# Linear attention and a gated feed-forward block on one core: the first stage's loads reordered over two DMA queues, and a second x tile transposed on TensorE

## Chip, core and metric

The kernel runs on one core of a Trainium2 chip. The metric is the device time of one execution in microseconds. The times given for a kernel are the median of several executions and their lowest and highest; a profile is of one execution, and its span runs from the first to the last instruction.

## What is computed

x is 2048 x 640 in bf16 (2048 tokens, width 640). A linear attention with 32 heads of 20 columns and a feed-forward block with 1728 hidden columns both read x, and a gate per token mixes them.

```python
g = sigmoid((x * gate_w).sum(-1))
q, k, v = split(x @ wqkv)                  # 640 columns each, 32 heads of 20
phi = lambda t: where(t > 0, t + 1, exp(t)) + 1e-6
kv  = per head: phi(k)^T @ v               # 20 x 20
z   = per head: sum over tokens of phi(k)
a   = (phi(q) @ kv) / (phi(q) . z + 1e-6) @ wo
b   = (gelu(x @ w_gate) * (x @ w_up)) @ w_down
out = g * a + (1 - g) * b
```

## The kernel before

**Tiles.** The tokens are cut into NT = 16 tiles of 128, the width 640 into KC = 5 pieces of 128. TensorE needs x with the width on the partitions, and so a transposed copy, xT. The key and query projections multiply one 128 x 128 piece of xT with the 640 key columns (wk) or the 640 query columns (wq) of the same piece of width, and sum over the five pieces in PSUM. A 641st query column holds gate_w, so that the query projection gives the gate's sum too.

**Order of the work.** There is no scheduler: each engine runs its instructions in the order in which the program text names them (class `_Plan`), and the plan puts a semaphore wait ahead of an instruction where its operands need one. A wait holds up everything that stands behind it on the same engine. Loads are issued by the sequencers of SP (`eng="sp"`) and of ACT (`eng="act"`), and each has a DMA queue of its own: q1 for SP, q10 for ACT.

**First stage (lines 363 to 535).** NXN = 1 tile of x is loaded as it is (`load_x`, L343) and transposed by TensorE (`T`, L439: five transposes against an identity into PSUM, from where VectorE copies them into xT, L443). All other tiles come through transposing DMAs (`load_xT`, L355), which SP issues. The `load_wk` and `load_wq` loads (L343) bring 160 KB each. SP's order is: x 0, wk 0, xT 1, wk 3, wk 4, xT 2, xT 3, wq 0 to 4, xT 4 to 15, then the bulk loads (the remaining untransposed x, the feed-forward weights, wv, wo). ACT's order is: a load of 16 rows of 8 bytes (`touch`, L368), wk 1, wk 2, an Exp on one column that brings the activation table in (L379), and gate_w (L381).

TensorE first runs matmuls on constants (`warm`, L425). Then the NQ = 4 first tiles have key and query done in units of their own: `KM(n, ks)` (L459 and L460) multiplies pieces ks of key unit n, with 512 and 128 columns, `QM(n, ks)` (L474 and L475) those of a query unit, with 512 and 129. Unit n uses PSUM banks `slot(n)`: (0, 1), (2, 3), (4, 5), (6, 7) in turn. TensorE's order is

```python
warm(5, 512); warm(1, 128)
T(0, [0], 7); T(0, [1, 2, 3, 4], 6)
warm(2, 128)
KM(0, [0]), KM(0, [1]), KM(0, [2]), KM(1, [0]), KM(1, [1]), KM(1, [2])
KM(0, [3]), KM(1, [3]); gate_col(); KM(0, [4]), KM(1, [4])
KM(2, ALLK), KM(3, ALLK)       # then the query units of the tiles 0 to 3
```

`gate_col` is one small matmul (L504) that turns gate_w into a column and a copy by VectorE (L506) into column 641 of wq; every `QM` waits for that copy. After each unit `phi1` (ACT, L484 and L488) and `phi2` (VectorE, L494 and L498) apply phi and free the unit's banks.

**Key and query of the other tiles (L538 to 574).** `KQ(i)` multiplies the five pieces of xT tile i with wk and wq side by side in three groups (512, 512 and 257 columns, L545) into banks 0 to 2 or 3 to 5, for i from NQ to 15, with phi on ACT (L555) and VectorE (L561, L564).

**After that** TensorE sums phi(k)^T x over all tiles (L602 to L617), runs the feed-forward's gate and up products (L706) with the small attention matrices in between, and ends with the output products (L859, L880). These parts are the same in both kernels.

Of the kernel before, what the change touches and what calls it, by code (L numbers as in the profile page):

```python
# [6 lines left out]
ACT = mybir.ActivationFunctionType  # L7
ALU = mybir.AluOpType
BF16 = mybir.dt.bfloat16
F32 = mybir.dt.float32  # L10
# [5 lines left out]
NT = S // 128  # L16
KC = D // 128
# [3 lines left out]
EPS = 1e-6  # L21
XW = 656

NXN = 1
NQ = 4


class _Res:
# [134 lines left out]
def bass_gated_mix__linear_attn_block__geglu_ffn__prompt_kernel(  # L163
# [63 lines left out]
    with (  # L227
# [8 lines left out]
        with contextlib.ExitStack() as stack:  # L236
            dma_sems = [stack.enter_context(nc.semaphore("s_in%d" % i)) for i in range(n_dma_in)]

            P = _Plan(["pe", "act", "dve", "pool", "sp"])
# [9 lines left out]
            def new_dma_key():  # L249
                k = "in%d" % dma_next[0]  # L250
                dma_next[0] += 1
                return k

            def v16(o, n):
                return pool[:, o:o + n]

            def v32(o, n):
                return pool[:, o:o + 2 * n].bitcast(F32)
# [38 lines left out]
            eg = v32(O_EG, 16)  # L297
# [3 lines left out]
            gw_sb = v16(O_GW, 128)  # L301
# [6 lines left out]
            r_xT = [P.sb("xT%d" % i, R_XT, R_XT + KC * S) for i in range(NT)]  # L308
            r_xTa = [P.sb("xTa%d" % i, R_XT, R_XT + S) for i in range(NXN)]
            r_wk = [P.sb("wk%d" % k, R_WK + k * WW, R_WK + k * WW + 640) for k in range(KC)]  # L310
# [25 lines left out]
            r_eg = [P.res("eg%d" % i) for i in range(NT)]  # L336
# [3 lines left out]
            r_gw = P.res("gw")  # L340
# [7 lines left out]
            def load_x(i, eng="sp"):  # L348
                dma_in(x_aug[:, i, 0:640], A_x[0, i * 128:(i + 1) * 128, :], [r_xn[i]], eng=eng)

            def load_wk(k, eng="sp", after=()):
                dma_in(wk[:, k, :], A_wqkv[k * 128:(k + 1) * 128, 640:1280], [r_wk[k]], reads=after, eng=eng)

            def load_xT(i, after=()):
                P.op("sp", lambda e: e.dma_start_transpose(xT[:, :, i * 128:(i + 1) * 128],  # L355
                                                           A_x[0, i * 128:(i + 1) * 128, :]),
                     reads=list(after), writes=[r_xT[i]], dma=new_dma_key())

            def load_wq(k, eng="sp"):
                dma_in(wq[:, k, 0:640], A_wqkv[k * 128:(k + 1) * 128, 0:640], [r_wq[k]], eng=eng)  # L360
# [4 lines left out]
                                                   base=0, channel_multiplier=1),  # L365
                 reads=[r_ones], writes=[r_ident])
            P.op("pool", lambda e: e.memset(v32(R_WO, NHC * 320), 0.0), reads=[r_ident], writes=[r_woz] + r_wo)
            P.op("act", lambda e: e.dma_start(touch[0:16, 0:4], A_wqkv[0:128:8, 640:644]),  # L368
                 writes=[P.res("touch")], dma=new_dma_key())
            load_x(0)  # L370
            load_wk(0)
            load_xT(1)
            load_wk(3)
            load_wk(4)
            load_wk(1, "act")
            load_wk(2, "act")

            zero = nc.const_aps.tensor(0.0, (128, 1), F32)
            P.op("act", lambda e: e.activation(eg[:, 0:1], zero, ACT.Exp), writes=[r_eg[0]])  # L379
            P.op("dve", lambda e: e.memset(gw_sb, 0.0), writes=[r_gw])  # L380
            dma_in(gw_sb[0:5, :], gate_w.rearrange("(k p) -> k p", p=128), [r_gw], eng="act")  # L381
            for i in range(2, NQ):
                load_xT(i)
            for k in range(KC):
                load_wq(k)
            for i in range(NQ, NT):
                load_xT(i)
            dma_in(x_aug[:, NXN:8, 0:640],
                   A_x[0, NXN * 128:8 * 128, :].rearrange("(i p) w -> p i w", p=128), r_xn[NXN:8])
            dma_in(x_aug[:, 8:NT, 0:640],  # L390
# [30 lines left out]
            def warm(count, n):  # L421
                def fn(e):
                    last = None
                    for w in range(count):
                        last = e.matmul(ps[:, 4, 0:n], one_l, one_r[:, 0:n], start=True, stop=True)  # L425
                    return last
                P.op("pe", fn, writes=[bank[4]])
# [7 lines left out]
            def T(i, ks, tb):  # L435
                def fn(e):
                    last = None
                    for n, k in enumerate(ks):
                        last = e.transpose(psb[:, tb, n * 128:(n + 1) * 128],  # L439
                                           x_aug[:, i, k * 128:(k + 1) * 128], ident)  # L440
                    return last
                P.op("pe", fn, reads=[r_xn[i], r_ident], writes=[bank[tb]])
                P.op("dve", lambda e: e.tensor_copy(  # L443
                    xT[:, ks[0]:ks[-1] + 1, i * 128:(i + 1) * 128],
                    psb[:, tb, 0:len(ks) * 128].rearrange("p (k s) -> p k s", k=len(ks))),
                    reads=[bank[tb]], writes=[r_xTa[i] if ks[0] == 0 else r_xT[i]])


            seq = [("k", i) for i in range(NQ)] + [("q", i) for i in range(NQ)]

            def KM(n, ks):
                i = seq[n][1]
                b0, b1 = slot(n)

                def fn(e):
                    last = None
                    for k in ks:
                        lhs = xT[:, k, i * 128:(i + 1) * 128]
                        e.matmul(ps[:, b0, :], lhs, wk[:, k, 0:512], start=(k == 0), stop=(k == KC - 1))  # L459
                        last = e.matmul(ps[:, b1, 0:128], lhs, wk[:, k, 512:640],  # L460
                                        start=(k == 0), stop=(k == KC - 1))
                    return last
                P.op("pe", fn, reads=[r_xTa[i] if i < NXN and ks == [0] else r_xT[i]] + [r_wk[k] for k in ks],
                     writes=[bank[b0], bank[b1]])

            def QM(n, ks):
                i = seq[n][1]
                b0, b1 = slot(n)

                def fn(e):  # L470
                    last = None
                    for k in ks:
                        lhs = xT[:, k, i * 128:(i + 1) * 128]
                        e.matmul(ps[:, b0, :], lhs, wq[:, k, 0:512], start=(k == 0), stop=(k == KC - 1))  # L474
                        last = e.matmul(ps[:, b1, 0:129], lhs, wq[:, k, 512:641],  # L475
                                        start=(k == 0), stop=(k == KC - 1))
                    return last
                P.op("pe", fn, reads=[r_xT[i], r_gcol] + [r_wq[k] for k in ks],
                     writes=[bank[b0], bank[b1]])

            def phi1(n):
                b0, b1 = slot(n)
                m = n % 4
                P.op("act", lambda e: e.activation(e_buf[m], ps_flat[:, b0 * 512:b0 * 512 + 640], ACT.Exp),  # L484
                     reads=[bank[b0], bank[b1]], writes=[r_e[m]])
                kind, i = seq[n]
                if kind == "q":
                    P.op("act", lambda e: e.activation(eg[:, i:i + 1], ps[:, b1, 128:129], ACT.Tanh, scale=0.5),  # L488
                         reads=[bank[b1]], writes=[r_eg[i]])

            def phi2(n):
                b0, b1 = slot(n)
                m = n % 4
                P.op("dve", lambda e: e.tensor_scalar(e_buf[m], e_buf[m], 1.0, EPS, ALU.min, ALU.add),  # L494
                     reads=[r_e[m]], writes=[r_e[m]])
                kind, i = seq[n]
                dst, r_dst = (pk[i], r_pk[i]) if kind == "k" else (pq[i], r_pq[i])
                P.op("dve", lambda e: e.scalar_tensor_tensor(  # L498
                    dst, ps_flat[:, b0 * 512:b0 * 512 + 640], 1.0 + EPS, e_buf[m], ALU.add, ALU.max),
                    reads=[bank[b0], bank[b1], r_e[m]], writes=[r_dst])  # L500
# [10 lines left out]
            warm(1, 128)  # L511
            T(0, [0], 7)
            T(0, [1, 2, 3, 4], 6)
            warm(2, 128)
            for k in range(3):
                KM(0, [k])
            for k in range(3):
                KM(1, [k])
            KM(0, [3])
            KM(1, [3])  # L520
            gate_col()
            KM(0, [4])
            KM(1, [4])
            ALLK = list(range(KC))
            for n in range(2 * NQ):
                if n in (2, 3):
                    KM(n, ALLK)
                if n == NQ:
                    for k in ALLK:
                        QM(NQ, [k])  # L530
                        QM(NQ + 1, [k])
                if n > NQ + 1:
                    QM(n, ALLK)
                phi1(n)
                phi2(n)


            def KQ(i):  # L538
                b = 3 * (i % 2)
# [405 lines left out]
```

## Time and profile before

| | |
|---|---|
| time, median of 3 executions | 273.71 us (273.53 to 273.76) |
| the profiled execution, its own time | 273.49 us |
| its span | 272.2 us |
| VectorE (DVE) busy | 140.9 us, 52% of the span |
| ScalarE (ACT) busy | 76.0 us, 28% |
| GpSimd (POOL) busy | 30.6 us, 11% |
| moved by queue q1, which SP issues | 23.05 MB |
| moved by queue q10, which ACT issues | 0.33 MB |

What lies around the span is 273.49 - 272.2 = 1.3 us. PE stands for TensorE's matmuls, PEld for its weight loads, which go on beside the matmuls; SPq and ACTq are the sequencers of SP and ACT that issue DMAs. In a timeline a row has its start, its duration, engine, line, operation, output <- input, shapes and count; the bracket tells how long the engine had been idle before it and what ended that idle time. The start-to-start distance of two matmuls is the time that the first takes of TensorE's stream; the durations overlap. A DMA's time to landing is counted from its issue to the last of its completion signals.

### The profile page before, as it was taken

Reading aid. Unit: us, or ns where it says so; the run is one execution under the profiler, and the core shown is the slowest. Engines: PE = TensorE matmul, PEld = TensorE weight load, DVE = VectorE, ACT = ScalarE, POOL = GpSimd, SP = SyncE. Lnnn points to the kernel's source line nnn. Section 1 sums busy time; section 2 is a strip of 40 time slices with the busy share of each in tenths; the row PEclk is TensorE's granted clock in tenths of the full one; section 3 lists DMA queues with packets and bytes.
Section 4 is the critical chain, followed back from the end, with each engine's and each line's share of the span. In section 5 each row is a group of like instructions: output and inputs, shape, how many; then the busy total and the mean of one; then the engine's idle time right before and its main releaser. Section 6 shows DMA issues by size and latency. Waiting matters only on the chain.

```text
span 272.2 us, 3462 instructions
## 1 busy us (share of the span) xinstructions
PE 267.0 (98%) x1366; PEld 127.2 (47%) x1392; DVE 140.9 (52%) x248; ACT 76.0 (28%) x132; POOL 30.6 (11%) x30
## 2 busy tenths in 40 slices
PE   7999999999999999999999999999999999999997
PEld 3555555544445454444444444444444444444444
DVE  1678989997234335999999999634110000000200
ACT  2455555210422453332222232224011122121021
POOL 6000000003240002242332421000000000000000
DMA  7976999610200011614121221262031110110221
GB/s 192 203 117 120 356 401 379 117 3 19 58 19 2 23 52 48 198 28 52 24 48 29 46 48 25 60 233 94 2 78 40 39 39 19 41 39 19 58 60 39
DMA packets 42680, 23.61 MB, mean 87 GB/s; under 512 B 32167, under 2 KB 41255, under 8 KB 42535
## 3 DMA queue, kind: packets, MB, share of 16 engines
q1 hardware_dynamic: 42333, 23.05, 32.2%
q10 hardware_dynamic: 330, 0.33, 0.4%
q8 instruction: 11, 0.18, 0.3%
q14 instruction: 6, 0.05, 0.1%
HBM read 13.67 MB, written 2.63 MB: 60 GB/s over the span
## 4 chain that ended last, share of the span: by engine, by line
PE 96%; DMA 1%; SPq 1%; issue 1%; DVE 0%
PE ps L706 41%; PE ps L880 23%; PE ps L545 12%; PE ps L602 6%; PE ps L859 4%; PE ps L684 2%; PE ps L474 2%; PE ps L827 2%; PE ps L605 1%; DMA pool<-in_A_x_dram 1%; PE ps L459 1%; PE ps L840 1%; SPq L343 1%; SPq L355 0%; PE ps L755 0%
## 5 line engine op out<-in xcount | busy, mean ns | idle before, releaser
L706 PE MATMUL ps<-pool 128*128 128x512 bf16 x509 | 112.8, 379 | 0.7 <-issue 0.2
L706 PEld LDWEIGHTS ps<-pool 128*128 128x128 bf16 x520 | 50.6, 98 | 60.3
L880 PE MATMUL ps<-pool 128*128 128x512 bf16 (+2 forms) x300 | 62.2, 366 | 0.5 <-issue 0.2
L712 ACT ACTIVATE pool<-ps 128x512 f32<-128x512 f32 x52 | 31.1, 597 | 72.8 <-PE ps L706 70.1
L714 DVE TENSOR_TENSOR pool<-ps,pool 128x512 bf16<-128x512 f32 x52 | 34.7, 688 | 31.1 <-PE ps L706 29.8
L880 PEld LDWEIGHTS ps<-pool 128*128 128x128 bf16 x306 | 29.2, 98 | 33.4 <-issue 0.4
L863 DVE TENSOR_TENSOR pool<-ps,pool 128x512 bf16<-128x512 f32 x4 | 2.8, 692 | 61.5 <-PE ps L859 59.4
L545 PE MATMUL ps<-pool 128*128 128x512 bf16 (+1 forms) x176 | 32.5, 343 | 0.2
L770 POOL TENSOR_TENSOR pool<-pool 128x640 f32<-128x640 bf16 x16 | 22.5, 1406 | 72.6 <-DVE pool L772 65.8
L887 ACT ACTIVATE pool<-ps,pool 128x512 bf16<-128x512 f32 (+1 forms) x16 | 10.9, 681 | 68.6 <-PE ps L880 68.6
L545 PEld LDWEIGHTS ps<-pool 128*128 128x128 bf16 x180 | 17.6, 98 | 15.0
L564 DVE SCALAR_TENSOR_TENSOR pool<-ps,pool 128x128 bf16<-128x128 f32 (+2 forms) x36 | 21.7, 603 | 2.1
L555 ACT ACTIVATE pool<-ps 128x640 bf16<-128x640 f32 x24 | 16.9, 704 | 15.8 <-DVE pool L564 9.3
L602 PE MATMUL ps<-pool 128*128 128x512 bf16 x76 | 19.2, 379 | 0.1
L780 DVE TENSOR_TENSOR pool<-pool 128x640 bf16<-128x640 bf16 x16 | 13.2, 825 | 0.6
L778 DVE TENSOR_SCALAR pool<-pool 128x32 f32<-128x32 f32 x16 | 12.8, 802 | 0.6
L772 DVE TENSOR_REDUCE pool<-pool 128x32 f32<-128x640 f32 x16 | 12.9, 807 | 0.0
L650 DVE TENSOR_TENSOR pool<-pool 128x640 f32<-128x640 f32 x14 | 11.6, 825 | 0.5
L859 PE MATMUL ps<-pool 128*128 128x512 bf16 x51 | 11.4, 379 | 0.0
L652 POOL PARTITION_ALL_REDUCE pool<-pool x1 | 4.0, 3972 | 60.2 <-DVE pool L650 60.2
L602 PEld LDWEIGHTS ps<-pool 128*128 128x128 bf16 x78 | 6.9, 98 | 7.3
L561 DVE TENSOR_SCALAR pool<-pool 128x640 bf16<-128x640 bf16 x24 | 7.8, 326 | 1.7 <-ACT pool L555 0.4
(73 smaller groups left out, 123.4 us busy)
## 6 DMA issues: line engine op xcount, KB each, us to landing
out_dram<-pool SPq DMA_DIRECT2D x19, 128.0 KB, 1.7
pool<-in_B_w_gate_dram SPq DMA_DIRECT2D x1, 2080.0 KB, 14.3
pool<-in_B_w_up_dram SPq DMA_DIRECT2D x1, 2080.0 KB, 18.4
pool<-in_A_wqkv_dram SPq DMA_DIRECT2D x8, 160.0 KB, 3.0
pool<-in_A_x_dram SPq DMA_DIRECT2D x1, 1280.0 KB, 9.3
pool<-in_A_x_dram SPq DMA_DIRECT2D x1, 1120.0 KB, 6.4
pool<-in_B_w_down_dram SPq DMA_DIRECT2D x1, 1120.0 KB, 6.2
pool<-omg_row SPq DMA_DIRECT2D x1, 1024.0 KB, 4.8
```

Source lines behind the costliest of these rows:

```text
L545: last = e.matmul(ps[:, b + p, 0:c1 - c0], xT[:, k, i * 128:(i + 1) * 128], wkq[:, k, c0:c1], start=(k == 0), stop=(k == KC - 1))
L555: P.op("act", lambda e: e.activation(e_buf[m], ps_flat[:, o:o + 640], ACT.Exp), reads=banks, writes=[r_e[m]])
L564: P.op("dve", lambda e, c0=c0, c1=c1: e.scalar_tensor_tensor(dst[:, c0:c1], ps_flat[:, o + c0:o + c1], 1.0 + EPS, e_buf[m][:, c0:c1], ALU. ...
L602: last = e.matmul(ps[:, b, :], pk[i][:, c * 128:(c + 1) * 128], x_aug[:, i, 0:512], start=(i == 0), stop=(i == NT - 1))
L706: last = e.matmul(ps[:, b, :], w[:, k, fc * 128:(fc + 1) * 128], xT[:, k, j * 512:(j + 1) * 512], start=(k == 0), stop=(k == KC - 1))
L712: P.op("act", lambda e: e.activation(ge[n], ps[:, gb, :], ACT.Gelu_apprx_tanh), reads=[bank[gb]], writes=[r_ge[n]])
L714: P.op("dve", lambda e: e.tensor_tensor(hT[fc][:, j * 512:(j + 1) * 512], ps[:, ub, :], ge[n], ALU.mult), reads=[bank[ub], r_ge[n]], write ...
L770: P.op("pool", lambda e: e.tensor_tensor(tmp[n], pq[i], z_b, ALU.mult), reads=[r_pq[i], r_zb], writes=[r_tmp[n]])
L772: P.op("dve", lambda e: e.tensor_reduce(den[n], tmp[n].rearrange("p (h d) -> p h d", h=32), AX.X, ALU.add), reads=[r_tmp[n]], writes=[r_de ...
L780: P.op("dve", lambda e: e.tensor_tensor(pq[i].rearrange("p (h d) -> p h d", h=32), pq[i].rearrange("p (h d) -> p h d", h=32), den[n].unsqu ...
L859: last = e.matmul(ps[:, b, :], wd[:, fc, 512:640], hT[fc][:, j * 512:(j + 1) * 512], start=False, stop=(fc == NFC - 2), skip_group_check=True)
L880: last = e.matmul(ps[:, pb, 0:c1 - c0], lhs, rhs, start=False, stop=(q == len(rows) - 1), skip_group_check=True)
```

## The change

The untransposed loads of x 0 and x 1, all five wk and all five wq are issued first, in the order of use and alternating between SP and ACT; the transposing DMAs come behind them, for the tiles 2 to 15. SP's order becomes x 0, wk 0, wk 2, wk 4, wq 1, wq 3, xT 2 to 15, bulk. ACT's becomes the Exp with its table, touch, x 1, wk 1, wk 3, gate_w, wq 0, wq 2, wq 4. Tile 1 is transposed by TensorE in one call `T(1, ...)`, which stands ahead of all `KM` units; the second `warm` goes. Only two tiles have separate key and query units (NQ = 2): `KQ` begins at tile 2. `gate_col` stands behind the last `KM`, directly ahead of the `QM` units.

```diff
-NXN = 1
-NQ = 4
+NXN = 2
+NQ = 2
...
+            zero = nc.const_aps.tensor(0.0, (128, 1), F32)
+            P.op("act", lambda e: e.activation(eg[:, 0:1], zero, ACT.Exp), writes=[r_eg[0]])
+            P.op("dve", lambda e: e.memset(gw_sb, 0.0), writes=[r_gw])
             P.op("act", lambda e: e.dma_start(touch[0:16, 0:4], A_wqkv[0:128:8, 640:644]),
                  writes=[P.res("touch")], dma=new_dma_key())
             load_x(0)
+            load_x(1, "act")
             load_wk(0)
-            load_xT(1)
-            load_wk(3)
+            load_wk(1, "act")
+            load_wk(2)
+            load_wk(3, "act")
             load_wk(4)
-            load_wk(1, "act")
-            load_wk(2, "act")
-
-            zero = nc.const_aps.tensor(0.0, (128, 1), F32)
-            P.op("act", lambda e: e.activation(eg[:, 0:1], zero, ACT.Exp), writes=[r_eg[0]])
-            P.op("dve", lambda e: e.memset(gw_sb, 0.0), writes=[r_gw])
             dma_in(gw_sb[0:5, :], gate_w.rearrange("(k p) -> k p", p=128), [r_gw], eng="act")
-            for i in range(2, NQ):
-                load_xT(i)
-            for k in range(KC):
-                load_wq(k)
-            for i in range(NQ, NT):
+            load_wq(0, "act")
+            load_wq(1)
+            load_wq(2, "act")
+            load_wq(3)
+            load_wq(4, "act")
+            for i in range(NXN, NT):
                 load_xT(i)
...
             T(0, [1, 2, 3, 4], 6)
-            warm(2, 128)
-            for k in range(3):
+            T(1, [0, 1, 2, 3, 4], 5)
+            KM(0, [0])
+            KM(0, [1])
+            KM(1, [0])
+            KM(1, [1])
+            for k in range(2, KC):
                 KM(0, [k])
-            for k in range(3):
                 KM(1, [k])
-            KM(0, [3])
-            KM(1, [3])
             gate_col()
-            KM(0, [4])
-            KM(1, [4])
             ALLK = list(range(KC))
-            for n in range(2 * NQ):
-                if n in (2, 3):
-                    KM(n, ALLK)
-                if n == NQ:
-                    for k in ALLK:
-                        QM(NQ, [k])
-                        QM(NQ + 1, [k])
-                if n > NQ + 1:
-                    QM(n, ALLK)
+            phi1(0)
+            phi2(0)
+            phi1(1)
+            phi2(1)
+            for k in ALLK:
+                QM(2, [k])
+                QM(3, [k])
+            for n in (2, 3):
                 phi1(n)
                 phi2(n)
```

## The prediction, made before the changed kernel had run

> **What bounds the kernel now.** The page first: shares of busy time, then the chain that ended last.
>
> ```profile
> PE 267.0 (98%) x1366; PEld 127.2 (47%) x1392; DVE 140.9 (52%) x248; ACT 76.0 (28%) x132; POOL 30.6 (11%) x30
> ...
> PE 96%; DMA 1%; SPq 1%; issue 1%; DVE 0%
> ```
>
> TensorE is the bound. Only 1 + 1 + 1% of the chain is DMA, SP's sequencer and issue, and the chain in order of time puts nearly all of that ahead of one point:
>
> ```profile
> 4.15 3.90 DMA pool<-in_A_x_dram
> 8.05 0.05 issue
> 8.10 0.39 PE ps L459
> ```
>
> That DMA is the transposing load of x tile 2. Behind 8.10 us the matmuls follow each other without a gap to the end. So the question is when TensorE, with as much work left as it has at 8.10, can start it in the new order. TensorE's timeline:
>
> ```profile
> 0.82 2.40 PE L425 MATMUL ps<-const-bfloat16-1.0 128*128 128x512 bf16 x6 [0.82 <-PEq L930]
> 3.02 0.74 PE L439 MATMUL ps<-pool 128*128 128x128 bf16 x5
> ...
> 4.45 0.43 PE L459 MATMUL ps<-pool 128*128 128x512 bf16 x1 [0.48 <-DMA pool<-in_A_wqkv_dram]
> ...
> 5.90 0.39 PE L459 MATMUL ps<-pool 128*128 128x512 bf16 x1 [0.42 <-DMA pool<-in_A_x_dram]
> ...
> 7.21 0.22 PE L460 MATMUL ps<-pool 128*128 128x128 bf16 x1
> 7.27 0.17 PE L504 MATMUL ps<-pool 128*128 128x5 bf16 x1
> 7.29 0.38 PE L459 MATMUL ps<-pool 128*128 128x512 bf16 x1
> ...
> 8.10 0.39 PE L459 MATMUL ps<-pool 128*128 128x512 bf16 x1
> ```
>
> The reader is to see three waits, on wk 0, xT 1 and xT 2. The brackets count only time with no matmul in the array; a 512 and a 128 column matmul take 0.272 of the stream (7.29 to 7.56), and so measured the waits are 0.68 (from 3.77, the end of `warm`), 0.58 and 0.26 us, though the last row has no bracket. The gate's matmul takes 0.03 us of the stream because matmuls of KM stand behind it. At 8.10 KM(0) and KM(1) are done. Left are KM(2), KM(3), four query units and KQ(4) to KQ(15): 16.27 - 8.10 = 8.17 us, then KQ. In the new order, after KM(0), KM(1) and the gate, two query units, KQ(2) and KQ(3) are left ahead of KQ(4): 2 x 1.36 + 2 x 32.67/12 = 8.17. The same. **The change is worth 8.10 minus the start S of the first QM**, if nothing later stalls.
>
> **When x 1 lands.** Now T(1) stands ahead of every KM on TensorE, and all ten KM calls wait behind it; wk 0 may be there, nothing uses it. x 1 has the place on ACT's queue that wk 1 had: second, behind touch, 160 KB. The DMA view of that issue alone (1.23 us), and of x 0's on SP (0.79):
>
> ```profile
> pool<-in_A_wqkv_dram ACTq DMA_DIRECT2D x1, 160.0 KB, 3.3
> ...
> pool<-in_A_x_dram SPq DMA_DIRECT2D x1, 160.0 KB, 2.2
> ```
>
> The Exp and its table load now stand ahead of ACT's loads:
>
> ```profile
> 2.20 1.28 ACT L379 ACT_TABLE_LOAD   x1 [2.20 <-issue]
> 2.27 0.57 ACTq L343 DMA_DIRECT2D pool<-in_gate_w_dram  x1
> ```
>
> gate_w was issued during the table load, so the sequencer doesn't wait for it; from wk 2's issue end (2.16) to 2.27 is 0.1 us, where loads otherwise follow at 0.04. Cost 0.06: x 1 is issued at 1.29. With 3.3 it lands at 4.56. SP's queue now competes. From 3.0 to 3.5 us both queues moved 65 packets each; from 3.5 SP's had little until its transposes, and ACT's last 60 packets of wk 1 had the 375 GB/s (293 packets per us) nearly alone: 0.2 us, which becomes 0.4 with wk 2 on SP. So 4.56 to 4.76; I take 4.65.
>
> **From x 1 to S.** First transpose 0.05 after landing (x 0: 2.97 by its last signal, 3.02). Four more spaced 0.107 at the clock of T(0), or 0.056 at the later one (7.21 to 7.27), the last lasting 0.31 or 0.22, then VectorE 0.03 later:
>
> ```profile
> 3.37 0.23 DVE L443 COPY pool<-ps 128x128 bf16<-128x128 bf16 x1 [2.39 <-PE ps L439]
> 3.79 0.42 DVE L443 COPY pool<-ps 128x512 bf16<-128x512 bf16 x1 [0.20 <-PE ps L439]
> 7.50 0.18 DVE L506 CAST pool<-ps 128x5 bf16<-128x5 f32 x1 [3.28 <-PE ps L504]
> ```
>
> The copy of 640 columns: 0.42 + 0.19 x 128/384 = 0.48. VectorE to TensorE isn't shown as a wait that ends last; bounds 0 and 0.21 (copy end 4.21, next weight load 4.42, released by wk 0); I take 0.07, nearest to the 0.03 to 0.1 of the other hand-overs. So KM(1, [0]) starts 0.05 + 0.22 + 0.22 + 0.03 + 0.48 + 0.07 = 1.07 behind landing at the later clock, 1.37 at the early one; I take 1.15. KM(0, [0]) and KM(0, [1]) lie inside that. Then 8 calls of 0.272 (5.90 to 6.18) = 2.18.
>
> Then the gate, whose cover is gone: VectorE's copy began 0.23 after the gate's matmul and took 0.18, QM waits for it (0.07): 0.48, during which TensorE has nothing; behind QM stand all queries and KQ.
>
> S = 4.65 + 1.15 + 2.18 + 0.48 = **8.46, which is 0.36 later than 8.10**. The waits of 0.58 and 0.26 and the 0.21 of `warm` go, but T(1), its copy and the gate's gap come, and the first wait, now for x 1, gets longer.
>
> **The other edits.** wk 1, third on ACT, is needed at 4.65 + 0.6; wk 2, in that place, landed at 4.96, now perhaps at 5.1. Hidden; S can't be below wk 1's landing + 0.05 + 9 x 0.272 + 0.48, which is 8.08. wk 3 and 4: 0.3 MB had moved by 3.25 us; x 0, x 1 and wk are 1.15 MB; the rest at 375 GB/s ends at 5.5, signals some 0.5 later, needed at 6.9. Two slices of 0.5 us, from 3.5 with loads on both queues and from 9.0 with wq on SP alone:
>
> ```profile
> DMA packets 190, 0.19 MB, mean 375 GB/s; under 512 B 48, under 2 KB 190, under 8 KB 190
> ...
> DMA packets 118, 0.13 MB, mean 269 GB/s; under 512 B 13, under 2 KB 118, under 8 KB 118
> ```
>
> At 269 wk 4 would be there at 6.9: still in time. (The Trainium skill, "DMA: Bandwidth & Descriptors", section "Issuing engines are not separate DMA queues", says that transfers of either sequencer run on the same 16 DMA engines and that a second issuer saves issue time alone. That speaks against the two queues; by it 269 would hold throughout, and the sum would be as it is.) wq 0 to 4: all 1.97 MB by 7.7 to 9.4, plus 0.5; wq 4 is needed at S + 4 x 0.54 = 10.6. xT 2 is issued at 0.79 + 6 x 0.46 = 3.55 and comes behind wq 3; 0.16 MB at the 239 GB/s of a slice full of transposes is 0.7, so 8.9 to 10.6; needed at S + 2.72 = 11.2. Later tiles come every 1.3 us, and KQ takes 2.72 each. The bulk loads move forward by some 3 us and nothing waits for them. Banks: KQ(2) needs those of KM(0), KM(1), whose phi on VectorE ends about S + 2.4. All at nothing.
>
> The profiled execution took 273.49 (span 272.2, 1.3 around it); 0.36 gives 273.85. The median is 0.22 above that execution: **274.1**.
>
> **Cases.** 0.2%, 0.55 us, is about what a measurement can tell from no change: S under 7.55 or over 8.65.
>
> A, the sum (0.56): x 1 at 4.56 to 4.76, with both clocks and hand-overs 0.1 to 0.8 late, 273.8 to 274.5. Within 0.2%: 0.34, slower 0.22.
>
> B (0.14): x 1 lands like x 0, 2.2 after issue, at 3.5. For it: same source, and x 0 shows what such a load can do. Against it: wk 0 (3.1) and wk 1 took much longer beside each other. Then wk 1 decides: S = 8.08, 273.7. Only if wk 1 too landed before 4.57 would it be faster by 0.2%: 0.05; same 0.09.
>
> C (0.18), slower: TensorE's clock. Warm matmuls of 512 columns stood 0.427 apart, later ones 0.216; the first KM, at 4.45, 0.265 ahead of the next. The rise came at about 4.5, 3.7 after the first matmul. Before, KM had waits of 0.58 and 0.26 to cover a late rise; the new order has none, idles from 3.6 to 4.65 and starts with transposes. If the count begins anew at 4.65, the clock rises at 8.35: 5.85 calls at 0.533 from 5.23, then 4.15 at 0.272: S = 9.48 + 0.48 = 9.96, +1.86, 275.6. Between, 0.49 per us; it decides from a rise at about 5.0 on. Against it: the idle stretch before was nearly as long (3.8 to 4.45).
>
> (The Trainium skill, "TensorE: Matmul & The Clock Gate", sections "What's actually happening" and "Part 4: PE-mode transpose", has the clock released after a busy window of some 3.4 us, and transposes not counted as busy. By that a missed window moves the rise to 7.9, and S, as an estimate, to 9.7; by the rise at 4.5 the sum stands.)
>
> D (0.12): the loads don't come sooner: weights and transposes share some 200 GB/s, as the 6.0 to 8.1 us stretch did with 166. 1.67 MB from 3.25 take 8.3, xT 2 another 0.7 + 0.5: 12.7 in place of 11.2, and TensorE waits 1.5 more: 275.6. Slower 0.10, same 0.02.
>
> Faster 0.05, same 0.34 + 0.09 + 0.02 = 0.45, slower 0.22 + 0.18 + 0.10 = 0.50. The range 273.4 to 275.4 leaves out the faster part of B and the ends of C and D, some 0.13.
>
> **What the changed profile would show.** T(1)'s first transpose at 4.6 to 4.8 with x 1 as releaser; KM(1, [0]) waiting for VectorE; KMs 0.272 apart, or 0.533 under C; the gate's matmul, then 0.45 us of nothing until L474 at about 8.5; no wait for xT or wq behind. Wrong if x 1 lands by 4, if KM waits for wk, or if KQ(2) waits for xT 2.

## The result, and the profile after

The changed kernel takes 275.37 us (median of 10 executions, 274.01 to 276.42), the kernel before 273.66 (10 executions, 273.53 to 274.85): ratio 1.0053, 95% interval 1.003 to 1.0076. It is slower by some 0.5%, and its executions scatter over 2.4 us where nine of ten before lie within 0.4. The profiled execution took 275.20, with a span of 273.9.

TensorE's share and the chain, from the page of the changed kernel:

```profile
PE 268.4 (98%) x1359; PEld 128.0 (47%) x1385; DVE 142.0 (52%) x251; ACT 75.9 (28%) x132; POOL 30.5 (11%) x30
...
PE 97%; DMA 1%; issue 1%; DVE 0%; ACT 0%
```

TensorE still bounds it, with 1.4 us more of "busy" time although its matmuls are fewer (1359 records for 1366): some of them must have taken longer. TensorE's timeline of the changed kernel shows which:

```profile
3.08 0.71 PE L439 MATMUL ps<-pool 128*128 128x128 bf16 x5
4.66 0.72 PE L439 MATMUL ps<-pool 128*128 128x128 bf16 x5 [0.87 <-DMA pool<-in_A_x_dram]
5.17 0.63 PE L459 MATMUL ps<-pool 128*128 128x512 bf16 x1
...
5.71 0.63 PE L459 MATMUL ps<-pool 128*128 128x512 bf16 x1
...
7.84 0.49 PE L459 MATMUL ps<-pool 128*128 128x512 bf16 x1
8.17 0.22 PE L460 MATMUL ps<-pool 128*128 128x128 bf16 x1
8.23 0.38 PE L459 MATMUL ps<-pool 128*128 128x512 bf16 x1
...
9.31 0.17 PE L504 MATMUL ps<-pool 128*128 128x5 bf16 x1
9.79 0.39 PE L474 MATMUL ps<-pool 128*128 128x512 bf16 x1 [0.30 <-DVE pool L506]
```

The KM calls start 0.54 apart (5.17, 5.71) until the one at 7.84, and 0.27 apart from 8.23 on. A 512-column matmul shows 0.63 us at the slow clock, 0.38 at the fast one, and the clock rose in the middle of the one at 7.84, which has 0.49. Worked out from starts, the rise was at 8.07; the trace's record of the granted clock has 8.06 (the expectations below say 7.9, from a first reading of the spacing). The last row is the gate's gap: 9.31 to 9.79. The first QM starts 9.79 - 8.10 = 1.69 later than the third KM did before, and the execution is 275.20 - 273.49 = 1.71 longer.

A second thing doesn't show in the chain. The DMA queues of the changed kernel from 7.5 to 10.5 us, with GB/s in 40 slices of 0.075:

```profile
DMA  9999999999392900000000100059999999398565
GB/s 335 304 290 300 259 184 184 157 89 61 85 72 55 61 17 34 17 34 17 34 17 17 34 20 20 20 38 106 75 75 109 126 164 109 38 147 79 58 92 130
DMA packets 670, 0.30 MB, mean 102 GB/s; under 512 B 535, under 2 KB 670, under 8 KB 670
...
q1 hardware_dynamic: 538, 0.15, 84.7%
q10 hardware_dynamic: 132, 0.15, 45.6%
```

The 16 engines are charged with 85 + 46 = 131% of their time for 0.30 MB: packets of both queues, transposes on q1 and wq on q10, take long beside each other. From 8.55 to 9.45 us next to nothing moves (at most 34 GB/s), and there the engines are charged with 7% of their time, so it isn't the engines that are short. wq 0 to 4 landed at 9.57, 8.65, 10.24, 9.75 and 11.91 us, xT 2 at 12.07. TensorE used wq 4 first at 11.97, in the ninth QM call, and xT 2 at 12.52:

```profile
11.97 0.38 PE L474 MATMUL ps<-pool 128*128 128x512 bf16 x1
...
12.52 0.59 PE L542 MATMUL ps<-pool 128*128 128x512 bf16 x2
```

So there are two theories. **Clock**: the late rise is the loss. **Loads**: wq 0 at 9.57 would have held the first QM back to 9.6 in any case, and wq 4 at 11.91 the ninth to 11.96, 0.01 ahead of where it started. They are tested against each other, and the gate's gap with them.

### The profile page after: what moved, and what is told of

It is laid out like the page before. It is cut to its first block, busy times and chain, and to the rows that moved or that the text cites. A ratio compares the mean times of both kernels' runs of the same rounds, so it can differ in the third digit from the quotient of the medians.

```text
span 273.9 us, 3454 instructions
## 1 busy us (share of the span) xinstructions
PE 268.4 (98%) x1359; PEld 128.0 (47%) x1385; DVE 142.0 (52%) x251; ACT 75.9 (28%) x132; POOL 30.5 (11%) x30
## 4 chain that ended last, share of the span: by engine, by line
PE 97%; DMA 1%; issue 1%; DVE 0%; ACT 0%
PE ps L703 41%; PE ps L877 23%; PE ps L542 14%; PE ps L599 6%; PE ps L856 4%; PE ps L681 2%; PE ps L824 2%; PE ps L602 1%; DMA pool<-in_A_x_dram 1%; PE ps L459 1%; PE ps L474 1%; PE ps L837 1%; PE ps L752 0%; PE ps L728 0%; PE ps L460 0%
## 5 line engine op out<-in xcount | busy, mean ns | idle before, releaser
L703 PEld LDWEIGHTS ps<-pool 128*128 128x128 bf16 x520 | 50.6, 98 | 60.2
L877 PEld LDWEIGHTS ps<-pool 128*128 128x128 bf16 x306 | 29.2, 98 | 33.4 <-issue 0.4
L542 PE MATMUL ps<-pool 128*128 128x512 bf16 (+1 forms) x206 | 37.9, 343 | 0.2
L542 PEld LDWEIGHTS ps<-pool 128*128 128x128 bf16 x210 | 20.5, 98 | 17.5
L561 DVE SCALAR_TENSOR_TENSOR pool<-ps,pool 128x128 bf16<-128x128 f32 (+2 forms) x42 | 25.3, 603 | 2.4
L552 ACT ACTIVATE pool<-ps 128x640 bf16<-128x640 f32 x28 | 19.7, 703 | 17.9 <-DVE pool L561 10.9
L599 PEld LDWEIGHTS ps<-pool 128*128 128x128 bf16 x78 | 7.0, 98 | 7.3
L558 DVE TENSOR_SCALAR pool<-pool 128x640 bf16<-128x640 bf16 x28 | 9.2, 327 | 1.5
```

What stands on the lines that cost most here:

```text
L542: last = e.matmul(ps[:, b + p, 0:c1 - c0], xT[:, k, i * 128:(i + 1) * 128], wkq[:, k, c0:c1], start=(k == 0), stop=(k == KC - 1))
L552: P.op("act", lambda e: e.activation(e_buf[m], ps_flat[:, o:o + 640], ACT.Exp), reads=banks, writes=[r_e[m]])
L561: P.op("dve", lambda e, c0=c0, c1=c1: e.scalar_tensor_tensor(dst[:, c0:c1], ps_flat[:, o + c0:o + c1], 1.0 + EPS, e_buf[m][:, c0:c1], ALU. ...
L599: last = e.matmul(ps[:, b, :], pk[i][:, c * 128:(c + 1) * 128], x_aug[:, i, 0:512], start=(i == 0), stop=(i == NT - 1))
L703: last = e.matmul(ps[:, b, :], w[:, k, fc * 128:(fc + 1) * 128], xT[:, k, j * 512:(j + 1) * 512], start=(k == 0), stop=(k == KC - 1))
L877: last = e.matmul(ps[:, pb, 0:c1 - c0], lhs, rhs, start=False, stop=(q == len(rows) - 1), skip_group_check=True)
```

## The experiments

In what follows S is the start of the first QM, or 2.72 us less than the start of KQ(2) where TensorE waits for that, or for the kernel before the start of the third KM. If nothing behind S matters, an execution takes 273.49 + S - 8.10.

**e1, constant matmuls while x 1 comes.**

```diff
+            warm(9, 128)
             T(1, [0, 1, 2, 3, 4], 5)
```

> The changed kernel with nine more constant matmuls of 128 columns (0.107 us each at the early clock) between the transposes of tile 0 and of tile 1, so that TensorE doesn't idle while x 1 comes. Clock theory (the late rise of TensorE's clock, at 7.9 us in place of 4.5, is what cost the time): the KM matmuls stand 0.27 apart from about 4.6 us on, the first QM starts at 8.5 and the time is some 1.3 us below the changed kernel's, about 274.1, 0.1 to 0.2% above before. Loads theory (wq 0 landed at 9.57, wq 4 at 11.91 and xT 2 at 12.07 us, so that TensorE would have had to wait there in any case): the clock rises early too, but the first QM waits for wq 0 until 9.6 and the last QM for wq 4 until 11.9; at most 0.2 us is gained, ratio to before about 1.005.

274.52 (274.07 to 275.19, 11 executions), ratio 1.0029 (1.0016 to 1.0042). Timeline:

```profile
6.27 0.31 PE L460 MATMUL ps<-pool 128*128 128x128 bf16 x1
6.38 0.44 PE L459 MATMUL ps<-pool 128*128 128x512 bf16 x1
6.65 0.22 PE L460 MATMUL ps<-pool 128*128 128x128 bf16 x1
...
9.08 0.39 PE L474 MATMUL ps<-pool 128*128 128x512 bf16 x1 [0.30 <-DVE pool L506]
```

The rise came at 6.50, within the call that starts at 6.38, and not at 4.5: without an idle stretch, and yet later than in the kernel before. S is 9.08, released by the gate's copy and not by wq 0, which landed at 7.87. The median fell by 0.85 from the changed kernel's, between the two expectations; the lower end of the spread stayed at 274.1, the upper fell from 276.4 to 275.2. So the clock costs, but its rise isn't a fixed time behind TensorE's first work.

**e2, the gate ahead of the last KM calls.**

```diff
             for k in range(2, KC):
+                if k == 4:
+                    gate_col()
                 KM(0, [k])
                 KM(1, [k])
-            gate_col()
```

> The changed kernel with the gate's matmul and copy ahead of the two last KM calls, as before the change, so that the 0.45 us gap ahead of the first QM goes. Clock theory: the clock still rises at 7.9 us, the first QM starts 0.45 sooner, at 9.35, and the time falls by 0.45, ratio to before about 1.0035. Loads theory: the first QM waits for wq 0 until 9.6, the last for wq 4 until 11.9: 0 to 0.2 us gained, ratio 1.0045 to 1.005.

275.36 (273.60 to 277.20, 12 executions), ratio 1.0057 (1.0034 to 1.008): no gain to be seen, and the widest spread so far, wider than the price sought. The profile shows why:

```profile
6.70 0.58 PE L459 MATMUL ps<-pool 128*128 128x512 bf16 x1 [0.78 <-DMA pool<-in_A_wqkv_dram]
...
9.86 0.59 PE L459 MATMUL ps<-pool 128*128 128x512 bf16 x1
10.29 0.22 PE L460 MATMUL ps<-pool 128*128 128x128 bf16 x1
```

The rise came at 10.28, and a late wk 1 (6.57) had held KM(0, [1]) back to 6.70. The gap ahead of the first QM had gone (10.86 to 10.91), but S is 10.91. As a price for the gate this run is inconclusive; e11 repeats it with the clock's part made small.

**e3, transposing DMAs held until wq has landed.**

```diff
             for i in range(NXN, NT):
-                load_xT(i)
+                load_xT(i, after=r_wq)
```

> The changed kernel with SP's first transposing DMA held until all five wq loads have landed. Theory that transposes beside plain loads of the other queue slow both (30 to 125 GB/s from 8.25 to 10.5 us): wq 0 to 4 land between 7 and 8.7 us at 340 to 375 GB/s, xT 2 lands 3 us behind the last of them, at about 11.5, ahead of its use at 12.5; the time is that of the changed kernel within 0.2 us, since the clock sets it. Rival (the slow stretch comes of something else, or of the number of loads in the queues): wq 4 lands at 11 to 12 all the same, xT 2 at 14 to 15, and TensorE waits 2 us or more for it: ratio to before 1.012 or more.

276.00 (274.74 to 278.07, 6 executions), ratio 1.0086 (1.0053 to 1.0119). wq 4 landed at 9.04 and no slow stretch came, so the transposes beside the loads of the other queue do make it. xT 2 landed at 11.96. The time was not that of the changed kernel within 0.2: in the profiled execution x 1 landed late, at 5.36, the clock rose at 4.06 all the same, and TensorE waited for xT 2: KQ(2) started at 12.10, 0.26 later than it would have come behind the first QM at 9.12. The other five executions were slower and have no profile; the hold trades one lateness for another.

**e4, the three edits together.** e1, e2 and e3 in one kernel.

> The three edits together: constant matmuls while x 1 comes, the gate ahead of the last KM calls, transposes held until wq is there. If clock, gate gap and slow loads together are the whole loss: first QM at 8.0 to 8.1 us, as before the change the third KM; then TensorE reaches KQ(2) at 10.8 and waits for xT 2 until about 11.5: 0.5 to 0.8 us above before, ratio 1.002 to 1.003. If the slow stretch of the loads doesn't come of the transposes, the first QM waits until 9.6 and KQ(2) until 14 or later: ratio 1.012 or more. If the filler doesn't bring the clock's rise forward, the first QM starts at 9.35: ratio about 1.005.

274.62 (274.41 to 275.78, 12 executions), ratio 1.0037 (1.002 to 1.0055). The rise was at 5.22, the first QM at 8.32, and KQ(2) waited:

```profile
11.99 0.59 PE L544 MATMUL ps<-pool 128*128 128x512 bf16 x2 [0.78 <-DMA pool<-in_A_x_dram]
```

The first part came out 0.2 to 0.3 later than the best case (wk 1 held one KM back by 0.34). The wait was longer than expected: behind a first QM at 8.32 KQ(2) could have started at 11.04, so the hold costs 0.95 of TensorE's stream, of which the bracket shows the 0.78 with no matmul in the array.

**e5, all wq on SP's queue ahead of the transposes**, no hold; filler and early gate as in e1 and e2.

```diff
-            load_wq(0, "act")
-            load_wq(1)
-            load_wq(2, "act")
-            load_wq(3)
-            load_wq(4, "act")
+            for k in range(KC):
+                load_wq(k)
```

> The changed kernel with constant matmuls ahead of tile 1's transposes and the gate ahead of the last KM calls, and in place of a wait for the transposing DMAs all five wq on SP's queue, ahead of them on the same ring; ACT's queue is empty by then. Theory that it is transposes of one queue beside plain loads of the other that slow both: no slow stretch, wq 4 lands at 9 to 9.5, xT 2 within 1.5 us behind it, at about 10.5, ahead of its use at 11, so the 0.78 us wait of the run with the three edits goes: time 273.8 to 274.0, ratio 1.001 to 1.0015. Rival (any transposes close to plain loads slow them): wq 4 lands at 10.5 or later and xT 2 at 12, ratio 1.003 or more.

273.76 (eleven of 12 executions 273.50 to 274.52, one of 613 from an unknown cause), ratio 1.0007 (0.9993 to 1.0021): level with the kernel before. The DMA view of the same stretch, 7.5 to 10.5 us:

```profile
DMA  8999999999979999999999645467999997320014
...
DMA packets 2169, 0.62 MB, mean 206 GB/s; under 512 B 2079, under 2 KB 2169, under 8 KB 2169
...
q1 hardware_dynamic: 2169, 0.62, 96.7%
```

More than twice the bytes, and no charge over 100% in this stretch. wq 4 landed at 8.58 and xT 2 at 9.19, 2.88 us earlier than in the changed kernel. S is 8.20, and KQ(2) started at 10.93 without a wait.

**e6, an order that might beat both.** As e5, but `warm(8, 128)`, KM(0, [0]) and KM(0, [1]) ahead of tile 1's transposes.

```diff
-            T(1, [0, 1, 2, 3, 4], 5)
+            warm(8, 128)
             KM(0, [0])
             KM(0, [1])
+            T(1, [0, 1, 2, 3, 4], 5)
```

> A version that might beat both: wq on SP's queue, constant matmuls until wk 0 is there, KM(0, [0]) and KM(0, [1]) ahead of tile 1's transposes, the gate ahead of the last KM calls. If the clock has risen by 4.5, the ten KM calls and the transposes (3.0 us) run from 4.45 on and the first QM starts at 7.6 to 7.7: 0.4 us under before, 273.2. If the clock rises later, each us costs 0.49: for rises spread evenly from 3.5 to 6.9 us some 0.4 on the mean, which gives the gain back: median 273.4 to 273.7, ratio 0.999 to 1.000, spread 273.1 to 274.3. Rival (x 1 and wk set the pace, not the clock): every execution at 273.2 to 273.4.

274.43 (274.22 to 274.98, 12 executions), ratio 1.0025 (1.001 to 1.004). Both expectations missed:

```profile
4.54 0.38 PE L456 MATMUL ps<-pool 128*128 128x512 bf16 x1
...
5.79 0.38 PE L456 MATMUL ps<-pool 128*128 128x512 bf16 x1 [0.82 <-DMA pool<-in_A_wqkv_dram]
...
7.09 0.39 PE L456 MATMUL ps<-pool 128*128 128x512 bf16 x1 [0.31 <-DVE pool L440]
```

The clock was up at 4.47. But KM(0, [1]) needs wk 1, which landed at 5.66, and the transposes that could have filled this time now stood behind it; the wait for their copy moved back with them. S is 9.03.

**e7 and e8, the two kernels again**, unedited, one profiled execution each.

> The changed kernel itself, for a second profile. Clock theory in its sharper form (the clock can rise only at points 3.41 us apart whose place differs from execution to execution, and does so when TensorE was busy for some three quarters of the stretch before): the rise is at another time than 7.9 us, anywhere from 3.5 to 10.4, and with a rise at R behind 5.2 the first QM starts at R + 0.53 + 0.2725 x (10 - (R - 5.17) / 0.533), or at wq 0's landing if that is later; the execution's time is 273.49 + that start - 8.10. Rival (the rise follows the kernel's own activity by a fixed time): again at 7.9 within 0.2 us.

> The kernel before itself, for a second profile. Clock theory: the rise is at another time than 4.5 us, but the third KM starts at 8.05 to 8.4 us all the same, since the waits for xT 1 and xT 2 leave room for slow matmuls: the time is 273.4 to 273.8 whatever the rise. Rival (a fixed delay): 4.5 again.

e7: rise at 8.17, S 9.89, 275.28 us. The formula gives 9.94 with its own KM start of 5.28; but the rise is so near that of the first profile (8.07) that this run alone does not exclude the rival. e8 does:

```profile
5.57 0.63 PE L459 MATMUL ps<-pool 128*128 128x512 bf16 x1
...
6.10 0.42 PE L459 MATMUL ps<-pool 128*128 128x512 bf16 x1
...
8.17 0.39 PE L459 MATMUL ps<-pool 128*128 128x512 bf16 x1
```

The same kernel, the same work, and the rise at 6.18, within the call at 6.10, in place of 4.55. The third KM started at 8.17 for all that, right behind xT 2 (8.12), and the execution took 273.60: the waits before 8.1 us had room for three slow calls.

**e9, e10, e11, one part of the change put back into e5 at a time**, so that each has its price with the others gone. e9: wq on both queues; e10: no filler; e11: the gate behind the last KM. The diffs are those of e5, e1 and e2, reversed.

> From the version with filler, early gate and wq on SP's queue (273.76, ratio 1.0007), wq goes back onto both queues beside the transposes, as in the changed kernel: the price of that part alone. With TensorE ready for QM at 8.2 us, needing wq 4 at 10.4 and xT 2 at 10.9: in the profiles of kernels with wq on both queues and no hold xT 2 landed at 12.07, 10.23, 11.44 and 10.99, so TensorE waits between 0 and 1.2 us, 0.45 on the mean: about 274.2, ratio 1.0015 to 1.004, a wide spread. Rival (the late loads were hidden, only the clock counted): 273.8, ratio 1.0007.

> The same version (filler, early gate, wq on SP's queue) without the filler: the price of the idle stretch between the transposes of tile 0 and tile 1 alone. Clock theory: some executions rise late (7 to 10.4 us), others by 5; 0.49 us for each us of late rise: median 0.5 to 1.2 us above 273.76, 274.3 to 275, ratio 1.0025 to 1.005, spread over 2 us. Rival (the clock's lateness is hidden behind wk and wq): 273.8.

> The same version with the gate behind the last KM call, as in the changed kernel: the price of that place alone. 0.48 us of nothing ahead of the first QM less the 0.03 that the gate's matmul takes in the stream: 274.2, ratio 1.0024. Rival (wq sets the first QM in any case): wq 0 landed at 6.78 there, so this would show as no difference, 273.8.

e9: 274.24 (273.62 to 274.94), ratio 1.0003 (0.9983 to 1.0023): a ratio below the expected one, and by it not told apart from e5 (0.9993 to 1.0021). Its median is the expected one and lies 0.48 above e5's; nine of its 12 executions took more than 273.85, three of e5's eleven did. In its profile wq 4 landed at 10.62 and xT 2 at 10.68, over a microsecond later than in e5, but they were needed at 10.8 and 11.3: hidden, with 0.2 and 0.6 us to spare. What this profile lost against e5's, S 8.59 for 8.20, was a wait for wk 1, which landed at 5.99 (5.54 in e5):

```profile
6.12 0.38 PE L459 MATMUL ps<-pool 128*128 128x512 bf16 x1 [0.39 <-DMA pool<-in_A_wqkv_dram]
```

So it isn't shown how the two queues cost 0.48 on the median, if they do.

e10: 274.99 (273.41 to 277.03), ratio 1.0041 (1.0013 to 1.0068), the median 1.23 above e5's. In its profile the clock makes the difference:

```profile
4.42 0.72 PE L436 MATMUL ps<-pool 128*128 128x128 bf16 x5 [0.44 <-DMA pool<-in_A_x_dram]
...
8.79 0.52 PE L456 MATMUL ps<-pool 128*128 128x512 bf16 x1
...
9.77 0.38 PE L471 MATMUL ps<-pool 128*128 128x512 bf16 x1
```

x 1 landed early (4.38), and the rise was at 9.07 all the same.

e11: 274.14 (274.04 to 274.53), ratio 1.0019 (1.0007 to 1.0031), the median 0.38 above e5's, where 0.45 was priced (the intervals of the two ratios overlap here too). Its profile has the gap, 0.47 from the gate's matmul to the first QM; the rest of S 8.91 for 8.20 is a later wk 1 (5.87 for 5.54):

```profile
8.44 0.17 PE L501 MATMUL ps<-pool 128*128 128x5 bf16 x1
8.91 0.39 PE L471 MATMUL ps<-pool 128*128 128x512 bf16 x1 [0.30 <-DVE pool L503]
```

**e12, another order that might win**: as e5, with `warm(8, 128)` and KM(0, [0]) ahead of tile 1's transposes, then KM(0, [2]), KM(0, [1]) and the rest of tile 1.

> A version that might beat the kernel before: the same loads, with KM(0, [0]) between filler and tile 1's transposes (wk 0 lands 0.2 us ahead of x 1), and wk 2 used ahead of wk 1, which lands later. With an early clock: KM(0, [0]) 4.45, transposes 4.75 to 5.0, KM(0, [2]) and KM(0, [1]) by 5.9, then seven calls to 7.85: first QM at 7.9, 273.3; with rises spread evenly from 3.5 to 6.9 some 0.3 later on the mean: median 273.4 to 273.7, ratio 0.9995 to 1.0005. Rival (bytes set the pace: wk 1 lands at 5.5 to 5.7 and nine calls follow): first QM at 8.1 or later whatever the clock, ratio 1.0005 or more.

273.89 (273.21 to 276.81, 12 executions), ratio 1.0006 (0.9982 to 1.003), S 8.39 with the rise at 5.47. The first KM after the transposes waited for wk 2 (5.79) and started at 5.92; with it nine calls and 0.03 for the gate were left: bytes set the pace here, as the rival had it. No version beat the kernel before.

## Why the prediction was right or wrong

Slower was forecast as the likelier side, and the measured 275.37 lies in the range, 0.03 from its upper end; the forecast itself, 274.1, is 1.3 too low. That the range holds the result is in part luck: the sum had 0.36 us for what came out as 1.71, and case C, which came about, stood in the prediction at 275.6, outside the range.

**The accounting held.** 273.49 + S - 8.10 against what the execution took:

| execution | rise | S | formula | took |
|---|---|---|---|---|
| changed | 8.07 | 9.79 | 275.18 | 275.20 |
| changed, again (e7) | 8.17 | 9.89 | 275.28 | 275.28 |
| before, again (e8) | 6.18 | 8.17 | 273.56 | 273.60 |
| e1 | 6.50 | 9.08 | 274.47 | 274.46 |
| e2 | 10.28 | 10.91 | 276.30 | 276.33 |
| e3 (KQ(2) waits) | 4.06 | 9.38 | 274.77 | 274.74 |
| e4 (KQ(2) waits) | 5.22 | 9.27 | 274.66 | 274.64 |
| e5 | 5.49 | 8.20 | 273.59 | 273.61 |
| e10 | 9.07 | 9.77 | 275.16 | 275.17 |

Within 0.04 us everywhere, in the four profiles left out here too: the whole difference between these kernels is made in the first 12 us, and nothing later gives any of it back.

**When x 1 lands**: 4.65 was taken, 4.62 came; the first transpose at 4.66 was right to 0.04, and so was pricing ACT's second place by wk 1's row.

**The gate**: 0.48 was taken, 9.31 to 9.79 came, and 0.47 in e11's profile.

**From x 1 to S, the step that failed**: "I take 1.15" and "8 calls of 0.272 = 2.18" both put the KM calls at the later clock. In the profile KM(1, [0]) came 1.62 behind landing (4.62 to 6.24), since the two calls in the gap took 0.53 each and hid the copy, and the eight calls from there took 3.07 (6.24 to 9.31). That is 0.47 + 0.89 = 1.36, the miss but for the 0.03 by which x 1 came sooner.

**Case C was what happened, and its weight of 0.18 was the error.** Its mechanism and place were right: before, the waits for xT 1 and xT 2 cover a rise as late as 6.18 (e8); without the filler TensorE has no such waits, and a late rise costs its full price (e7, e10). Its condition was too narrow. "If the count begins anew" made a late rise a question of whether the idle stretch resets something, and the nearly equal idle stretch of the kernel before was held against it. One profile of before can't show that the same program has its rise at 4.55 in one execution and at 6.18 in another. The estimate from the Trainium skill, "TensorE: Matmul & The Clock Gate", section "What's actually happening", S at 9.7, was the closest number in the prediction. That is luck in part: its rise at 7.9 is one window behind the 4.5 of another execution, and e8 shows that this place is not fixed.

**Case D, half.** The lateness was there: wq 0 to 4 by 11.91 and xT 2 at 12.07, past both of the bounds given (9.4 + 0.5 and 10.6). But its cause is not that weights and transposes share some 200 GB/s on any queue: on one queue (e5) they come by 9.2. In the first profile the late clock hid the late loads, but only just. The loads alone would have put the ninth QM call at 11.96 and so S at 9.78 (wq 4's landing at 11.91, 0.05 for the hand-over, less 2.18 for the eight calls ahead); the clock and the gate alone come to 9.79. That the two agree is chance, and this profile can't tell them apart. In e7 wq 0, landed at 8.70, would have let QM start at 8.75 and S was 9.89: there the clock and the gate make the loss.

**What the loss is made of.** Above the kernel before that ran beside them the medians stand at 1.71 us for the changed kernel, 0.97 with the filler (e1), 0.60 with the early gate as well (e9) and 0.18 with all wq on SP's queue too (e5). So the clock is the largest part, 0.74 here and 1.17 between e5 and e10; the gate is some 0.3 to 0.4, and the two queues 0.4. These sizes are read off medians: the intervals of neighbouring runs overlap, and only the whole way from the changed kernel to e5 is clear of them.

Open: e9 did not settle what the two queues cost by themselves; some executions of the kernel before took 275.2 to 275.5 (10 of 97 in all, 6 of the 35 beside e9 to e12), which a rise too late for its waits would explain, but none of those has a profile; and why packets of the two queues hold each other up isn't shown.

## What to carry to other kernels

A wait can pay for something: those for xT 1 and xT 2 were the room in which matmuls ran at the slow clock, and taking them away showed the clock. Before a start-up sequence is shortened, price its matmuls at the slow clock as well as the fast, keep TensorE busy while the first loads come, and keep small matmul-copy-matmul chains away from the ends of stages. Let transposing DMAs follow the plain loads on the same queue, not run beside those of another: the loads come earlier by it (e5), whether or not it pays in time.

## What the runs showed of the hardware

**The clock rises on a grid.** In the profiles that carry a record of the granted clock it is full from the rise for 266.24 us (changed kernel, e2, e7, e10) or 269.65 us (e3, e4, e6): 78 and 79 times 3.413 us. In every profile (the rise worked out from the starts where there is no record) TensorE's start-to-start occupancy in the 3.41 us ahead of the rise was 76% or more (79.9% before, 79.1% in e3, 76.1% in e8, 91 to 100% in the others), and in the full stretches of 3.41 us before that, which brought no rise, 69% at most (66.9% in the changed kernel, 63.9% in e7, 68.7% in e2 and e10, 64.2% in e1). If such a share decides, it lies between 69 and 76%; no run set the share to a chosen value. The place of the grid differs between executions of one kernel (e8). The changed kernel's idle 0.87 us puts it below that share for some places of the grid, and then a further 3.4 us run slow. The Trainium skill, "TensorE: Matmul & The Clock Gate", section "What's actually happening", has a window of 3413 ns that runs free of the kernel; these records agree. Section "Part 4: PE-mode transpose" says that transposes don't count as busy in the same way. These runs speak against it: without the transposes e8's stretch ahead of the rise has 61%, and one of e2's that brought none 64%; with them the order is right, 76 and 69%.

**Transposes on one queue and plain loads on the other slow each other.** wq 4 landed at 11.91, 10.12, 11.23, 10.86 and 10.62 us in the five profiles with wq on both queues beside the transposes, and at 8.58 to 8.94 in the five with wq ahead of them on SP's queue; xT 2 at 10.23 to 12.07 and at 9.19 to 9.53. With the transposes held until wq was there (e3, e4) wq 4 landed at 9.04 and 8.82 from both queues. A charge over 100% alone is no sign of two queues: in the kernel before q1 by itself is charged with 127% from 4.5 to 5.0 us, at 239 GB/s, while it moves mostly transposes.
